# Batch 0 of an attention-plus-MLP kernel: v's cast and q's first normalisation on GpSimd, q and x by head pairs, q's late rows in three pieces

## The chip, the cores and the metric

One core of one Trainium2 chip runs the whole program. The time is the device time of one execution in microseconds (us); before the change its median is 297.52 us. The engines are named as in the profile: PE is TensorE's matmul side and PEld its weight loads, DVE is VectorE, ACT is ScalarE, POOL is GpSimd, and SP is SyncE, which in this kernel only issues DMAs. Each engine takes its instructions in the order of the program.

## The reference

For 8 batches, 8 heads, 576 rows and 64 features, two softmaxes and two small products make x, and a two-layer network with a leaky ReLU follows. Here it is, cut to what is computed:

```python
q_s = exp(q - max(q, axis=-1));  q_s = q_s / (sum(q_s, axis=-1) + 1e-09)   # over the 64 features
k_s = exp(k - max(k, axis=2));   k_s = k_s / (sum(k_s, axis=2) + 1e-09)    # over the 576 rows
kv  = einsum('bhsd,bhse->bhde', k_s, v)
x   = einsum('bhsd,bhde->bhse', q_s, kv).transpose(0, 2, 1, 3).reshape(4608, 512)
h   = x @ w_in                     # 512 x 2048
out = maximum(0.01 * h, h) @ w_out # 2048 x 512
```

## The kernel before, in words

**Layout.** A head's 576 rows are taken as 64 places (`L`) of 9 rows each (`R`). Two heads fill the 128 partitions, and four such `HL` slots hold the batch, so a batch of q, k or v is a tile of 128 x 4 x 9 x 64 in float32. The tokens of a batch are kept in the order r, l, so the first 256 of batch 0's 576 tokens are the rows r = 0 to 3 (`RA`), and the next 256 the rows 4 to 7. x is kept transposed, as `xT`: four blocks of 128 features (a block is a pair of slots `gg` of one partition half `hh`; its number is 2·hh + gg), each with all 4608 tokens.

**The main part.** The tokens go through the network in 9 tiles of 512. For a tile, layer 1 (`layer1`, L452) makes 16 blocks `ph` of 128 hidden features, each from four matmuls over the four blocks of `xT`. ACT applies the leaky ReLU from PSUM to `g` (`leaky`, L461), and layer 2 (`layer2`, L473) makes four outputs `pout` of 128 tokens from 16 matmuls each. In tile 0 a `ph` holds two hidden blocks of 256 tokens, so its layer 1 has 128 matmuls of 256 columns.

**The attention of a batch.** DVE takes maxima (k by a tree, L162, and across partitions; q along the features, L226), DVE or POOL subtracts them (L195, L256), ACT takes the exponential (L203, L264), DVE sums and normalises q (L273, L280), v is cast to bf16 into `vb` (L215), PE makes the key-value products (`kv`, L295), DVE scales them into `kd`, q is transposed (on PE with `q_transpose`, L389, in batches 0 and 1, by DMA later), and `attend` (L412) makes the blocks of x with a copy into `xT`. The work of batches 1 to 7 is hung as hooks (`at(t, u, ...)`) on the matmul groups of an earlier tile, so each engine's order is written out by hand.

**Batch 0** comes ahead of everything, in this order: the loads, q's rows `RA` with a maximum and 16 small exponentials that also give the sums (`q_first`, L239), k's maxima by way of PE, two casts of v on ACT (L213), key-value products, q's transposes, and the first two blocks of x for 256 tokens. `wake(n)` puts n matmuls on zeros (L324) into PE's stream. Then DVE takes the maxima of q's late rows (`R1` is rows 4 and 5, `R2` is rows 6 to 8), and POOL subtracts them (L256).

**Queues.** SP loads q, k and v in the order of use. POOL issues the loads of the weights, which are cast to bf16 on the way: `load_w_in(0)` and `load_w_in(1)` are four pieces each (L133), `load_w_out` five pieces (L140). They are put off by small copies into `gate` that read a tile which must have landed: `w_in` first waits for k's second half (L509), then for its subtraction (L534), and `w_out` waits for the first half of batch 1's k (L564). SP in turn is held by `hold_sync` (L504), a tiny DMA that reads a piece of a weight: batch 1's loads wait for the fifth piece of `w_in`.

**PSUM.** Nearly every PSUM tile comes from one pool of six banks (`psB_pool`), so a new `ph` needs an earlier tile's reader, often a `leaky` on ACT, to be through.

**Tile 0 before.** Four `ph` tiles are begun on `xT`'s blocks 0 and 2, `attend` makes blocks 1 and 3, and then the groups are finished one by one:

```python
attend(0, [1, 3], 0, 256, nc.scalar)
for half in range(2):
    for j in range(0, NF, 2):
        ...
            layer1(j + i, ph[:, i], 256 * half, 256, part, i == 0, i == 1)
            if i == 1:
                leaky(g_sb[j // 2][:, :, 256 * half : 256 * half + 256], ph)
            run(0, 16 * half + j + i)
```

The late rows' exponentials hang on the groups j = 3 and j = 5, so in ACT's stream two `leaky` stand ahead of the first.

Of the kernel before, what the change touches and what calls it, by code (L numbers as in the profile page):

```python
# [25 lines left out]
def kernel(  # L26
# [201 lines left out]
    def q_first(b, rs):  # L228

        n = rs.stop - rs.start  # L230
        nmax = small_pool.tile([P, HL, n], FP32, name="nmax")
        qsum = small_pool.tile([P, n, HL], FP32, name="qsum")
        for hs in (slice(0, 2), slice(2, 4)):
# [3 lines left out]
            for h in range(hs.start, hs.stop):  # L237
                for r in range(n):
                    nc.scalar.activation(  # L239
                        out=st[b]["qe"][:, rs.start + r, h],  # L240
                        in_=st[b]["q"][:, h, rs.start + r],
                        func=AF.Exp,
                        bias=nmax[:, h, r : r + 1],
                        accum_out=qsum[:, r, h : h + 1],
                    )
        st[b]["qsum"] = qsum

    def q_first_rec(b, rs):
        n = rs.stop - rs.start
        st[b]["qrec", rs.start] = qrec = small_pool.tile([P, n, HL], FP32, name="qrec")  # L250
        nc.vector.reciprocal(out=qrec, in_=st[b]["qsum"])

    def q_sub(eng, b, rs):
        n = rs.stop - rs.start
# [67 lines left out]
    def wake(n):  # L322
        for i in range(n):
            nc.tensor.matmul(  # L324
                wake_ps, lhsT=zero[:, 0:P], rhs=zero, start=(i == 0), stop=(i == n - 1)
            )

    def k_max_pe(b, i):
        ps = psB_pool.tile([P, 2, L], FP32, name="kT", tag=BANK_TAG)
        nc.tensor.matmul(  # L330
            ps.rearrange("c h l -> c (h l)"),
            lhsT=st[b]["kmax"][:, 2 * i : 2 * i + 2].rearrange("p h d -> p (h d)"),
            rhs=identf,
            is_transpose=True,
        )
        st[b]["kT", i] = ps
# [154 lines left out]
            fn()  # L491

    H0, H1 = slice(0, 2), slice(2, 4)

    def load_all(b):
        whole = [(ALLH, ALLR)]
# [34 lines left out]
    v_cast(nc.scalar, 0, 0)  # L531
    v_cast(nc.scalar, 0, 1)
    k_sub_ps(0, 1)
    nc.gpsimd.tensor_copy(out=gate[:, 0:1], in_=st[0]["k"][:, HL - 1, R - 1, D - 1 : D])  # L534
    load_w_in(1)
    k_exp(0, H1)
    q_first_rec(0, RA)
    q_norm(0, RA)
    kv_pair(0, 0)
    wake(4)  # L540
    q_transpose(0, 0, 4)
    kv_pair(0, 1)
    for hh in range(2):
        kd_rec(0, 0, hh)
        kd_one(nc.vector, 0, 0, hh)
    q_keep(nc.scalar, 0, 0, 4, slice(0, 4, 2))
    q_keep(nc.vector, 0, 0, 4, slice(1, 4, 2))
    attend(0, [0, 2], 0, 256, nc.scalar)
    wake(3)
    kd_rec(0, 1, 0)  # L550
    kd_rec(0, 1, 1)
    kd_one(nc.vector, 0, 1, 0)
    kd_one(nc.vector, 0, 1, 1)
# [19 lines left out]
    at(0, 11, lambda: q_transpose(0, 4, 2), lambda: q_keep(nc.vector, 0, 4, 2))  # L573
    at(0, 13, lambda: q_transpose(0, 6, 3), lambda: q_keep(nc.vector, 0, 6, 3))
    at(0, 15, lambda: attend(0, [0, 2], 256, 256, nc.scalar))
    at(0, 15, lambda: attend(0, [1, 3], 256, 256, nc.vector))
    at(0, 17, lambda: attend(0, [0, 1, 2, 3], 512, 64, nc.scalar))
    at(0, 15, lambda: k_begin(1), lambda: q_begin(1), lambda: k_tree(1, H0), lambda: k_tree(1, H1))
    at(0, 15, lambda: k_allmax(1), lambda: k_sub(nc.gpsimd, 1, H0), lambda: k_sub(nc.vector, 1, H1))
    at(0, 15, lambda: q_max(1, RA), lambda: q_sub(nc.gpsimd, 1, RA))  # L580
    at(0, 15, lambda: q_max(1, RB), lambda: q_sub(nc.gpsimd, 1, RB))
    at(0, 29, lambda: k_exp(1, H1))
    at(0, 31, lambda: k_exp(1, H0), lambda: v_cast(nc.scalar, 1, 0))
    at(0, 33, lambda: q_exp(1, RA), lambda: q_sum(1, RA), lambda: q_norm(1, RA))
    at(0, 33, lambda: v_cast(nc.scalar, 1, 1), lambda: q_exp(1, RB))
    at(0, 38, lambda: kv(1), lambda: kd_make(1), lambda: q_sum(1, RB), lambda: q_norm(1, RB))
    at(0, 41, lambda: q_transpose(1, 0, 2), lambda: q_keep(nc.scalar, 1, 0, 2))
    at(0, 42, lambda: q_transpose(1, 2, 2), lambda: q_keep(nc.scalar, 1, 2, 2))
    at(0, 45, lambda: q_transpose(1, 4, 3), lambda: q_keep(nc.scalar, 1, 4, 3))
    at(0, 46, lambda: q_transpose(1, 7, 2), lambda: q_keep(nc.scalar, 1, 7, 2))  # L590
# [8 lines left out]
    def plan(b, o):  # L599
        t = b - 2  # L600
        at(t, o, lambda: k_begin(b), lambda: q_begin(b), lambda: k_tree(b, ALLH))
        at(t, o + 3, lambda: k_allmax(b), lambda: k_sub(nc.gpsimd, b, ALLH))
        at(t, o + 7, lambda: q_max(b, ALLR), lambda: q_sub(nc.gpsimd, b, ALLR))
        at(t, o + 11, lambda: k_exp(b, ALLH))
        at(t, o + 12, lambda: v_cast(nc.gpsimd, b, 0), lambda: v_cast(nc.gpsimd, b, 1))
        at(t, o + 16, lambda: q_exp(b, ALLR))
        at(t, o + 18, lambda: q_sum(b, ALLR))
        at(t, o + 21, lambda: q_norm(b, ALLR))
        kvu, pu = o + 25, o + (33 if b == 3 else 34)
        at(t, kvu, lambda: kv(b))  # L610
        at(t, kvu + 1, lambda: kd_make(b))
        at(t, o + 22, lambda: q_turn(b))
        for i in range(8):
            at(t, pu + i // 2, lambda i=i: attend_x(b, i // 2, XR[i % 2], nc.scalar))


    def plan2():
        b = 2
        at(1, 0, lambda: k_begin(b), lambda: q_begin(b), lambda: k_tree(b, ALLH))
        at(1, 3, lambda: k_allmax(b))  # L620
        at(1, 6, lambda: k_sub(nc.vector, b, H0), lambda: k_sub(nc.vector, b, H1))
# [7 lines left out]
        at(1, 21, lambda: kv(b))  # L629
        at(1, 22, lambda: kd_make(b))  # L630
        for i in range(8):
            at(1, 28 + i // 2, lambda i=i: attend_x(b, i % 4, XR[i // 4], nc.scalar))

    plan2()
    for b in range(3, B):
# [4 lines left out]
        return [g_pool.tile([P, 2, TT], BF16, name="gj") for _ in range(NF // 2)]  # L640

    g_sb = g_tiles()
    begun = []
    for j in range(0, 8, 2):
        ph = psB_pool.tile([P, 2, 256], FP32, name="ph", tag=BANK_TAG)
        for i in range(2):
            layer1(j + i, ph[:, i], 0, 256, slice(0, 2), i == 0)
        begun.append(ph)
    attend(0, [1, 3], 0, 256, nc.scalar)
    for half in range(2):  # L650
        for j in range(0, NF, 2):
            part = slice(2, 4) if begun else slice(0, 4)
            ph = begun.pop(0) if begun else psB_pool.tile([P, 2, 256], FP32, name="ph", tag=BANK_TAG)
            for i in range(2):
                layer1(j + i, ph[:, i], 256 * half, 256, part, i == 0, i == 1)
                if i == 1:
                    leaky(g_sb[j // 2][:, :, 256 * half : 256 * half + 256], ph)
                run(0, 16 * half + j + i)
# [66 lines left out]
```

## Time and profile before

| | us |
|---|---|
| median of the runs | 297.52 |
| lowest run | 296.36 |
| span of the profiled execution | 293.0 |
| PE busy in it | 278.8 |
| PE busy on zeros (L324, 26 matmuls) | 8.9 |
| ACT busy, DVE busy, POOL busy | 150.8, 144.9, 85.6 |
| tile 0: layer 1 begins, layer 2 begins | 17.05, 36.14 |
| tile 1: layer 1 begins | 54.28 |

The span runs from the first to the last instruction of one execution, whose own time is not listed apart from it. The median is 4.5 us above the span. A row of the timeline gives the start, the duration, the engine, the line, what is written from what, and in brackets the idle time before it with what ended that. A row that ends in x16 merges 16 instructions. A row of the waits view gives who waited for whom, the total, how often, and the longest.

### The profile page before, as it was taken

The numbers are of one execution on the slowest core, as the hardware profiler recorded it, in microseconds if no ns is written. First come the engines' busy times: TensorE is split into PE (matmuls) and PEld (weight loads), VectorE is DVE, ScalarE is ACT, GpSimd is POOL, SyncE is SP. The second block draws the span as 40 slices with busy tenths as digits, with TensorE's granted clock in tenths as the row PEclk, the third lists the DMA queues.
The fourth block names the chain that finished last, engine by engine and source line by source line (L and its number), as shares of the span: only waits on it lengthen the run. The fifth ranks groups of instructions, "written<-read, shape, count | busy, mean of one in ns | idle before, by whom it ended". The sixth has DMA issues, their size and how long they took to land.

```text
span 293.0 us, 4255 instructions
## 1 busy us (share of the span) xinstructions
PE 278.8 (95%) x1634; PEld 139.1 (47%) x1661; DVE 144.9 (49%) x240; ACT 150.8 (51%) x272; POOL 85.6 (29%) x61
## 2 busy tenths in 40 slices
PE   6596999999999999999999999999999999999995
PEld 2265845444544455454445544544455444444443
DVE  3947957885491597189367455735440200110011
ACT  4956682777058605951695338532854066007500
POOL 4645280025029307802920292029300000000000
PEclk9999999999999999999999999999999999999999
DMA  7999999694729553874399138923141310131032
GB/s 258 307 211 387 247 191 400 160 345 152 135 55 326 196 116 91 273 266 88 70 326 276 36 72 289 294 55 72 38 81 38 72 36 1 38 72 36 0 72 73
DMA packets 36580, 45.76 MB, mean 156 GB/s; under 512 B 15952, under 2 KB 19280, under 8 KB 36560
## 3 DMA queue, kind: packets, MB, share of 16 engines
q1 hardware_dynamic: 33120, 41.16, 47.4%
q0 software_dynamic: 3280, 4.20, 8.2%
q8 instruction: 13, 0.21, 0.3%
q10 hardware_dynamic: 160, 0.13, 0.1%
q14 instruction: 7, 0.06, 0.1%
HBM read 36.70 MB, written 9.44 MB: 157 GB/s over the span
## 4 chain that ended last, share of the span: by engine, by line
PE 84%; DMA 3%; DVE 3%; ACT 2%; POOL 2%; issue 1%; POOLq 0%; ACTq 0%
PE pout L473 40%; PE ph L452 39%; DMA w_in_sb<-in_moe_w_in_dram 3%; PE pkv L295 3%; PE po L440 2%; POOL k_raw L195 1%; DVE t L162 1%; ACT vb L213 1%; DVE k_raw L356 1%; ACT xT L422 1%; PE psum_qt L389 1%; POOL w_in_sb L133 0%; ACT qe L264 0%; DVE xT L424 0%; DVE m L179 0%
## 5 line engine op out<-in xcount | busy, mean ns | idle before, releaser
L452 PE MATMUL ph<-xT,w_in_sb 128*128 128x512 bf16 (+1 forms) x626 | 127.1, 357 | 4.3 <-DMA w_in_sb<-in_moe_w_in_dram 1.9
L473 PE MATMUL pout<-w_out_sb,gj 128*128 128x512 bf16 (+2 forms) x580 | 129.1, 373 | 0.9 <-issue 0.5
L461 ACT ACTIVATE gj<-ph 128x512 bf16<-128x512 f32 x144 | 82.5, 604 | 58.5 <-PE ph L452 57.9
L452 PEld LDWEIGHTS <-w_in_sb 128*128 128x128 bf16 x640 | 62.0, 98 | 66.1 <-issue 5.5
L473 PEld LDWEIGHTS <-gj 128*128 128x128 bf16 x592 | 56.9, 98 | 61.6
L467 DVE COPY out_sb<-pout 128x512 f32<-128x512 f32 (+1 forms) x34 | 22.7, 675 | 90.7 <-PE pout L473 82.1
L195 POOL TENSOR_TENSOR k_raw<-k_raw,kall 128x2304 f32<-128x2304 f32 (+1 forms) x6 | 29.1, 4844 | 86.2 <-DVE kall L187 55.8
L273 DVE TENSOR_REDUCE qsum<-qe 128x36 f32<-128x2304 bf16 (+4 forms) x11 | 19.8, 1800 | 39.5 <-ACT qe L264 39.5
L256 POOL TENSOR_TENSOR q_raw<-q_raw,qmax 128x2304 f32<-128x2304 f32 (+4 forms) x11 | 31.1, 2839 | 23.5 <-DVE qmax L226 23.5
L446 ACT CAST xT<-po 128x320 bf16<-128x320 f32 (+1 forms) x48 | 16.8, 402 | 40.0 <-PE po L440 40.0
L203 ACT ACTIVATE ke<-k_raw 128x2304 bf16<-128x2304 f32 (+2 forms) x11 | 17.5, 1595 | 9.7 <-POOL k_raw L195 9.4
L280 DVE TENSOR_TENSOR qe<-qe,qrec 128x2304 bf16<-128x2304 bf16 (+4 forms) x12 | 21.1, 1758 | 0.4
L226 DVE TENSOR_REDUCE qmax<-q_raw 128x36 f32<-128x2304 f32 (+4 forms) x11 | 19.4, 1788 | 0.0
L264 ACT ACTIVATE qe<-q_raw 128x2304 bf16<-128x2304 f32 (+4 forms) x11 | 16.9, 1535 | 0.0
L215 POOL CAST vb<-v_raw 128x1152 bf16<-128x1152 f32 x12 | 13.4, 1151 | 0.0
L467 ACT COPY out_sb<-pout 128x512 f32<-128x512 f32 (+1 forms) x3 | 1.6, 549 | 17.5 <-PE pout L473 17.5
L162 DVE TENSOR_TENSOR t<-k_raw 128x1024 f32<-128x1024 f32 (+1 forms) x10 | 10.1, 1010 | 0.4 <-DMA k_raw<-in_k_dram 0.2
L324 PE MATMUL pout<-zero 128*128 128x512 bf16 x26 | 8.9, 469 | 1.4 <-POOL zero L101 1.3
L162 DVE TENSOR_TENSOR t<-t 128x256 f32<-128x256 f32 (+2 forms) x20 | 9.6, 478 | 0.7
L440 PE MATMUL po<-qX,kd 128*128 128x320 bf16 (+1 forms) x48 | 9.8, 286 | 0.1
L295 PEld LDWEIGHTS <-ke 64*128 64x128 bf16 x252 | 7.2, 93 | 3.2 <-ACT gj L461 1.7
L295 PE MATMUL pkv<-vb,ke 64*128 64x129 bf16 x252 | 8.5, 216 | 0.1
(55 smaller groups left out, 103.5 us busy)
## 6 DMA issues: line engine op xcount, KB each, us to landing
out_dram<-out_sb SPq DMA_DIRECT2D x70, 128.0 KB, 2.4
q_raw<-in_q_dram SPq DMA_DIRECT2D x7, 1152.0 KB, 8.2
v_raw<-in_v_dram SPq DMA_DIRECT2D x7, 1152.0 KB, 11.0
k_raw<-in_k_dram SPq DMA_DIRECT2D x6, 1152.0 KB, 5.8
k_raw<-in_k_dram SPq DMA_DIRECT2D x4, 576.0 KB, 5.6
w_in_sb<-in_moe_w_in_dram POOLq DMA_DIRECT2D x8, 256.0 KB, 7.4
w_out_sb<-in_moe_w_out_dram POOLq DMA_DIRECT2D x3, 512.0 KB, 12.2
v_raw<-in_v_dram SPq DMA_DIRECT2D x2, 576.0 KB, 7.4
```

What stands on the lines that cost most here:

```text
L162: nc.vector.tensor_tensor(out=o, in0=i0, in1=i1, op=ALU.max)
L195: eng.tensor_tensor(out=ks, in0=ks, in1=st[b]["kall"][:, hs].unsqueeze(2).to_broadcast([P, n, R, D]), op=ALU.subtract,)
L203: nc.scalar.activation(out=st[b]["ke"][:, :, hs].rearrange("p r h d -> p h r d"), in_=st[b]["k"][:, hs], func=AF.Exp,)
L226: nc.vector.tensor_reduce(out=m, in_=st[b]["q"][:, :, rs], axis=AX.X, op=ALU.max)
L256: eng.tensor_tensor(out=qs, in0=qs, in1=st[b]["qmax", rs.start].unsqueeze(3).to_broadcast([P, HL, n, D]), op=ALU.subtract,)
L273: nc.vector.reduce_sum(out=qsum, in_=st[b]["qe"][:, rs], axis=AX.X)
L280: nc.vector.tensor_tensor(out=qes, in0=qes, in1=st[b]["qrec", rs.start].unsqueeze(3).to_broadcast([P, n, HL, D]), op=ALU.mult,)
L295: nc.tensor.matmul(pkv[hh][:, gg, 0:129], lhsT=st[b]["ke"][rows, r, 2 * gg : 2 * gg + 2].rearrange("p h d -> p (h d)"), rhs=vb2[b % 2][row ...
L452: nc.tensor.matmul(ph, lhsT=w_in_sb[:, cb, j * P : (j + 1) * P], rhs=xT[:, cb, c0 : c0 + n], start=(i == 0 and first), stop=(i == NB - 1 a ...
L461: nc.scalar.activation(out=o, in_=ph, func=AF.Prelu, alpha=LEAKY_SLOPE)
L467: copy(out=out_sb, in_=pout)
L473: nc.tensor.matmul(pout, lhsT=g_sb[j // 2][:, j % 2, tsub * P : (tsub + 1) * P], rhs=w_out_sb[:, j, os], start=(j == 0), stop=(j == NF - 1),)
```

## The change

The change concerns batches 0 to 3; the other hooks stay.

- v's two casts of batch 0 go from ACT to POOL, behind a `gate` copy that waits for k's last maximum.
- q's rows `RA` are normalised by head pairs: one reciprocal each on DVE, one multiplication each on POOL, where one reciprocal and one multiplication on DVE stood. They are also transposed, kept and attended by pairs.
- The first `w_in` gate waits for k's first half instead of its second. `load_w_in(1)` stands behind the casts and multiplications on POOL.
- `hold_sync` reads a piece of block 1 instead of block 0, so SP waits for the seventh `w_in` piece.
- Tile 0's first half is begun in two groups of four `ph`, part by part. Between parts stand the attends of blocks 1 and 3, the late rows' maxima and subtractions (`x1`), and two transposes.
- The late rows are cut in three (4 and 5, 6 and 7, 8). Their exponentials hang on j = 0, 3 and 13.
- Of batches 1 to 3, casts, exponentials, key-value products and attends move by some hooks. Zero matmuls go from 27 to 23.

The diff, cut to its core:

```diff
-    R1, R2 = slice(4, 6), slice(6, R)
+    R1, R2, R3 = slice(4, 6), slice(6, 8), slice(8, R)
...
+    def q_first_rec(b, gg):
+        st[b]["qrec2", gg] = qrec = small_pool.tile([P, RA.stop, 2], FP32, name="qrec2")
+        nc.vector.reciprocal(out=qrec, in_=st[b]["qsum", gg])
+
+    def q_first_norm(eng, b, gg):
+        qes = st[b]["qe"][:, RA, 2 * gg : 2 * gg + 2]
+        eng.tensor_tensor(
+            out=qes,
+            in0=qes,
+            in1=st[b]["qrec2", gg].unsqueeze(3).to_broadcast([P, RA.stop, 2, D]),
+            op=ALU.mult,
+        )
...
-    nc.gpsimd.tensor_copy(out=gate[:, 0:1], in_=st[0]["k"][:, HL - 1, R - 1, D - 1 : D])
+    nc.gpsimd.tensor_copy(out=gate[:, 0:1], in_=st[0]["k"][:, 1, R - 1, D - 1 : D])
     load_w_in(0)
...
+    nc.gpsimd.tensor_copy(out=gate[:, 0:1], in_=st[0]["kmax"][:, HL - 1, D - 1 : D])
+    v_cast(nc.gpsimd, 0, 0)
+    v_cast(nc.gpsimd, 0, 1)
...
-    wake(2)
+    wake(3)
+    q_first_rec(0, 0)
+    q_first_norm(nc.gpsimd, 0, 0)
     k_sub_ps(0, 0, HB)
     k_exp(0, slice(1, 2))
-    v_cast(nc.scalar, 0, 0)
-    v_cast(nc.scalar, 0, 1)
+    q_first_rec(0, 1)
+    q_first_norm(nc.gpsimd, 0, 1)
+    load_w_in(1)
     k_sub_ps(0, 1)
...
+    q_turn_first(0, 0)
+    q_keep_first(nc.vector, 0, 0)
...
+    attend(0, [0], 0, 256, nc.scalar)
     kv_pair(0, 1)
+    attend(0, [2], 0, 256, nc.scalar)
+    q_turn_first(0, 1)
+    q_keep_first(nc.scalar, 0, 1)
...
-    q_max(0, R1)
-    q_sub(nc.gpsimd, 0, R1)
-    q_max(0, R2)
-    q_sub(nc.gpsimd, 0, R2)
...
-    hold_sync(0, w_in_sb[0:1, 0, F - 128 : F])
+    hold_sync(0, w_in_sb[0:1, 1, F - 128 : F])
     st[1]["k"] = load(k, 1, "k_raw", [(H0, ALLR), (H1, ALLR)])
...
     nc.gpsimd.tensor_copy(out=gate[:, 0:1], in_=st[1]["k"][:, 0, 0, 0:1])
     for j0, j1 in ((0, 2), (2, 4), (4, 8), (8, 12), (12, 16)):
         load_w_out(slice(j0, j1))
...
-    at(0, 3, lambda: q_exp(0, R1), lambda: q_sum(0, R1), lambda: q_norm(0, R1))
-    at(0, 5, lambda: q_exp(0, R2), lambda: q_sum(0, R2), lambda: q_norm(0, R2))
...
+    def q_rest(rs):
+        q_exp(0, rs)
+        q_sum(0, rs)
+        q_norm(0, rs)
+
+    at(0, 0, lambda: q_rest(R1))
+    at(0, 3, lambda: q_rest(R2))
+    at(0, 13, lambda: attend(0, [0, 2], 256, 256, nc.scalar))
+    at(0, 13, lambda: attend(0, [1, 3], 256, 256, nc.vector))
+    at(0, 13, lambda: q_rest(R3))
+    at(0, 17, lambda: q_transpose(0, 8, 1), lambda: q_keep(nc.scalar, 0, 8, 1))
...
-        at(0, 47, lambda i=i: attend(1, [i // 2], 288 * (i % 2), 288, nc.scalar))
+        at(0, (45, 45, 46, 46, 46, 47, 47, 47)[i], lambda i=i: attend(1, [GS[i // 2]], 288 * (i % 2), 288, nc.scalar))
...
+    def begin(js, parts):
+        phs = [psB_pool.tile([P, 2, 256], FP32, name="ph", tag=BANK_TAG) for _ in js]
+        for i, between in parts:
+            for j, ph in zip(js, phs):
+                for h in range(2):
+                    layer1(j + h, ph[:, h], 0, 256, slice(i, i + 1), h == 0, False)
+            for fn in between:
+                fn()
+        return phs
+
+    def end(j, ph, half, part, first):
+        for h in range(2):
+            layer1(j + h, ph[:, h], 256 * half, 256, part, first and h == 0, h == 1)
+            if h == 1:
+                leaky(g_sb[j // 2][:, :, 256 * half : 256 * half + 256], ph)
+            run(0, 16 * half + j + h)
+
+    def x1():
+        attend(0, [1], 0, 256, nc.scalar)
+        attend(0, [3], 0, 256, nc.vector)
+        for rs in (R1, R2, R3):
+            q_max(0, rs)
+            q_sub(nc.gpsimd, 0, rs)
+
+    t1 = (lambda: q_transpose(0, 4, 2), lambda: q_keep(nc.scalar, 0, 4, 2))
+    t2 = (lambda: q_transpose(0, 6, 2), lambda: q_keep(nc.vector, 0, 6, 2))
+    for j0, parts in ((0, ((0, (x1,)), (1, ()))), (8, ((0, t1), (1, t2)))):
+        js = range(j0, j0 + 8, 2)
+        for j, ph in zip(js, begin(js, parts)):
+            end(j, ph, 0, slice(2, 4), False)
+    for j in range(0, NF, 2):
+        end(j, psB_pool.tile([P, 2, 256], FP32, name="ph", tag=BANK_TAG), 1, slice(0, 4), True)
```

More of the change, by code (lines that the diff above doesn't have):

```diff
@@ L231, in q_first @@
         nmax = small_pool.tile([P, HL, n], FP32, name="nmax")
-        qsum = small_pool.tile([P, n, HL], FP32, name="qsum")
-        for hs in (slice(0, 2), slice(2, 4)):
+        for gg in range(2):
+            hs = slice(2 * gg, 2 * gg + 2)
+            st[b]["qsum", gg] = qsum = small_pool.tile([P, n, 2], FP32, name="qsum2")
             nc.vector.tensor_reduce(
@@ L236, in q_first, with q_turn_first, q_keep_first @@
             )
-            for h in range(hs.start, hs.stop):
+            for h in range(2):
                 for r in range(n):
                     nc.scalar.activation(
-                        out=st[b]["qe"][:, rs.start + r, h],
-                        in_=st[b]["q"][:, h, rs.start + r],
+                        out=st[b]["qe"][:, rs.start + r, 2 * gg + h],
+                        in_=st[b]["q"][:, 2 * gg + h, rs.start + r],
                         func=AF.Exp,
-                        bias=nmax[:, h, r : r + 1],
+                        bias=nmax[:, 2 * gg + h, r : r + 1],
                         accum_out=qsum[:, r, h : h + 1],
                     )
[L246 to L251, printed above, removed]
+    def q_first_rec(b, gg):
[9 more added lines that the diff above has]
+        )
+    def q_turn_first(b, gg):
+        n = RA.stop
+        ps = psB_pool.tile([P, 2, n, L], BF16, name="psum_q2", tag=BANK_TAG)
+        for r in range(n):
+            nc.tensor.matmul(
+                ps[:, :, r],
+                lhsT=st[b]["qe"][:, r, 2 * gg : 2 * gg + 2].rearrange("p h d -> p (h d)"),
+                rhs=ident,
+                is_transpose=True,
+                start=(r == 0),
+                stop=(r == n - 1),
+            )
+        st[b]["ps2", gg] = ps
+    def q_keep_first(eng, b, gg):
+        o, i = st[b]["qT"][:, gg::2, RA], st[b]["ps2", gg]
+        if eng is nc.scalar:
+            eng.copy(out=o, in_=i)
+        else:
+            eng.tensor_copy(out=o, in_=i)
     def q_sub(eng, b, rs):
@@ L493 @@
     H0, H1 = slice(0, 2), slice(2, 4)
+    GS = (0, 2, 1, 3)
     def load_all(b):
@@ L527 @@
     k_all_pe(0, 1)
[L528 removed]
+    wake(3)
+    q_first_rec(0, 0)
+    q_first_norm(nc.gpsimd, 0, 0)
     k_sub_ps(0, 0, HB)
     k_exp(0, slice(1, 2))
[L531 to L532 removed]
+    q_first_rec(0, 1)
+    q_first_norm(nc.gpsimd, 0, 1)
+    load_w_in(1)
     k_sub_ps(0, 1)
[L534 to L535 removed]
     k_exp(0, H1)
[L537 to L538 removed]
     kv_pair(0, 0)
[L540 to L541 removed]
+    wake(2)
+    kd_rec(0, 0, 0)
+    kd_one(nc.vector, 0, 0, 0)
+    q_turn_first(0, 0)
+    q_keep_first(nc.vector, 0, 0)
+    kd_rec(0, 0, 1)
+    kd_one(nc.vector, 0, 0, 1)
+    attend(0, [0], 0, 256, nc.scalar)
     kv_pair(0, 1)
+    attend(0, [2], 0, 256, nc.scalar)
+    q_turn_first(0, 1)
+    q_keep_first(nc.scalar, 0, 1)
     for hh in range(2):
[L544 to L553, printed above, removed]
[L554 to L560 removed]
+        kd_rec(0, 1, hh)
+        kd_one(nc.vector, 0, 1, hh)
+    hold_sync(0, w_in_sb[0:1, 1, F - 128 : F])
     st[1]["k"] = load(k, 1, "k_raw", [(H0, ALLR), (H1, ALLR)])
@@ L591 @@
+    at(0, 33, lambda: q_sum(1, RB))
+    at(0, 41, lambda: kv(1))
+    at(0, 41, lambda: q_norm(1, RB), lambda: kd_make(1))
+    for r0 in (0, 2):
+        at(0, 41, lambda r0=r0: q_transpose(1, r0, 2), lambda r0=r0: q_keep(nc.scalar, 1, r0, 2))
+    for r0, n in ((4, 3), (7, 2)):
+        at(0, 43, lambda r0=r0, n=n: q_transpose(1, r0, n), lambda r0=r0, n=n: q_keep(nc.scalar, 1, r0, n))
     for i in range(8):
-        at(0, 47, lambda i=i: attend(1, [i // 2], 288 * (i % 2), 288, nc.scalar))
+        at(0, (45, 45, 46, 46, 46, 47, 47, 47)[i], lambda i=i: attend(1, [GS[i // 2]], 288 * (i % 2), 288, nc.scalar))
@@ L642 @@
     g_sb = g_tiles()
[L643 to L658, printed above, removed]
+    def begin(js, parts):
[8 more added lines that the diff above has]
+    def end(j, ph, half, part, first):
+        for h in range(2):
+            layer1(j + h, ph[:, h], 256 * half, 256, part, first and h == 0, h == 1)
[16 more added lines that the diff above has]
+        end(j, psB_pool.tile([P, 2, 256], FP32, name="ph", tag=BANK_TAG), 1, slice(0, 4), True)
     pout = [psO_pool.tile([P, O], FP32, name="pout") for _ in range(2)]
```

26 lines of the change are left out of this document (8 added, 18 removed).

## The prediction

> **What bounds the kernel now.** I read the page first, then the chain by line, then PE's waits and the timeline of the first 55 us.
>
> ```profile
> span 293.0 us, 4255 instructions
> PE 278.8 (95%) x1634; PEld 139.1 (47%) x1661; DVE 144.9 (49%) x240; ACT 150.8 (51%) x272; POOL 85.6 (29%) x61
> PE 84%; DMA 3%; DVE 3%; ACT 2%; POOL 2%; issue 1%; POOLq 0%; ACTq 0%
> ```
>
> PE carries the end: 278.8 of 293.0 us busy, and 84% of the chain. Whatever delays PE after layer 1 has begun (17.05) is added to the end one for one, unless a later wait of PE absorbs it. PE's waits from 16 to 45 us are few:
>
> ```profile
> PE ph L452 <- DMA w_in_sb<-in_moe_w_in_dram: 1.9, 1, 1.9
> PE ph L452 <- ACT xT L422: 1.4, 2, 0.7
> PE pout L473 <- issue: 0.2, 1, 0.2
> ```
>
> So 3.5 us is all that a better order could win there. The timeline shows in which order POOL and ACT serve this stretch:
>
> ```profile
> 16.41 0.58 ACT L422 CAST xT<-po 128x512 bf16<-128x512 f32 x1 [0.47 <-PE po L412]
> ...
> 17.80 2.47 POOL L256 TENSOR_TENSOR q_raw<-q_raw,qmax 128x512 f32<-128x512 f32 x2 [2.54 <-DVE qmax L226]
> ...
> 19.37 0.62 SPq L504 DMA_DIRECT2D held<-w_in_sb  x1
> ...
> 20.03 1.08 SPq L79 DMA_DIRECT2D k_raw<-in_k_dram  x2
> 20.48 1.08 ACT L461 ACTIVATE gj<-ph 128x512 bf16<-128x512 f32 x2 [0.69 <-PE ph L452]
> ...
> 21.45 0.63 ACT L264 ACTIVATE qe<-q_raw 128x512 bf16<-128x512 f32 x1
> ...
> 23.89 1.69 PE L452 MATMUL ph<-xT,w_in_sb 128*128 128x256 bf16 x14 [1.92 <-DMA w_in_sb<-in_moe_w_in_dram]
> ...
> 25.51 0.41 POOL L564 COPY gate<-k_raw 128x1 f32<-128x1 f32 x1 [5.24 <-DMA k_raw<-in_k_dram]
> ...
> 25.97 3.71 POOL L140 DMA_DIRECT2D w_out_sb<-in_moe_w_out_dram  x5
> ```
>
> The reader is to see POOL's order: the late rows' subtractions at 17.80, then 5.24 us of waiting for batch 1's k, then the w_out loads until 29.68. ACT takes two leaky ahead of the first late exponential (21.45).
>
> **The change part by part.** Times are on the clock of this one execution; its span is 293.0, the median 297.52, so I carry 4.5 us over.
>
> *Up to layer 1.* ACT loses two casts (2 x 1.14), DVE a multiplication of 1.22 us; POOL gets two casts (1.15 each, the L215 row), two multiplications, and a second gate copy (0.19 to 0.41). k's last maximum ends at 9.88, so the casts end near 12.5. Before, the first key-value product waited 1.44 us for v, until 13.22; now it starts at about 12.6. A multiplication of 512 elements per partition in bf16 on POOL is not in the trace: DVE's takes 0.69, POOL's subtraction of 128x512 in float32 1.04; and POOL's k subtraction of 1152 took 3.73 beside a DVE subtraction, against 5.07 for 2304, so 1.47 times longer, which gives 1.53. I take 1.04, the same engine and size; the ends are 0.69 and 1.53. The second multiplication ends at 14.6 (13.9 to 15.6). The two transposes, copies (0.42, 0.58) and attends by pairs then let layer 1 begin near 16.1 instead of 17.05. The GPSIMD Engine Reference (Trainium skill, 8. Key points) says GpSimd contends with VectorE instructions that have two SBUF inputs; by it the end at 1.53 would hold, and the 3.73 us row agrees. These 0.9 us are worth nothing to the end, since PE next waits for weights or for ACT. In the same way DVE's second reciprocal (0.16 to 0.25) and the extra PSUM tiles cost nothing: that wait covers them, and without it they would take at most 0.5 us off the 0.9.
>
> *w_in.* The second four loads are issued from 14.6 instead of 12.88, behind the casts and multiplications. Before, SP's hold went out at 19.37, when the fifth piece landed; the seventh, issued at 14.04, landed 7.9 us later, at 21.9. The shortest landing of a load of this size is 3.9 us (q's first), so a fifth piece issued at 14.6 to 15.6 can land at 18.5 to 19.5: the stream stays full and the seventh still lands near 22.0 (up to 23.0). The new hold waits for it; its row and the next put k's load 0.66 later, at 22.7. The k load took 5.4 behind w_in and q's first load 3.9; I take 4.2, as one w_in piece is still ahead. Batch 1's k lands at 26.9 (25.9 to 28.5) instead of 25.4. On SP's queue batch 1's q and v stand behind it and move by the same 1.5 to 2.6 us, as do w_out's landings, which share the DMA engines, and behind them batch 2's loads, held by a w_out piece. Layer 2 comes later by more than that (below) and batch 2 is first touched in tile 1, so this costs nothing; if layer 2 were not late, w_out's first pieces would be the next thing PE waits for.
>
> *POOL's queue.* This part decides. The late rows' subtractions used to stand ahead of the gate copy. `x1` is called from tile 0's loop, so they now stand behind the gate and the five w_out loads. From the gate to the end of the loads took 4.17 us (25.51 to 29.68), so R1's subtraction starts at 26.9 + 4.2 = 31.1, ends at 32.1, and ACT's exponential (0.63) ends at 32.8.
>
> *ACT's queue.* R1's exponential now hangs on j = 0 and stands ahead of the first leaky. ACT is idle from about 17.7 on, and all leaky wait behind it; the first ends at 33.4 (0.60). DVE waits as well, with its sum of R1; nothing behind it is due yet.
>
> *PE.* It goes on without ACT as long as PSUM has banks: 32 matmuls of the first group, and after w_in's sixth piece (20.6) four more of the second. The third `ph` of that group needs the bank that the first leaky frees. PE stands from about 21.2 to 33.45, 12.2 us, where before it stood 1.92.
>
> *From there to layer 2.* Of 128 matmuls 92 are left: 0.109 each (56 in 6.28 less the last one's tail) is 10.0. Ten transposes at 0.06 and the late attends (4 x 0.11, 4 x 0.03) are 1.2. Short waits: R1's normalisation (0.69 + 0.20 + 0.69 after 32.8) holds its transposes by 0.5; xT after the attends costs 0.7 as at 29.04; R3's short chain 0.7. Together 1.9. Zero in, this gives 46.5.
>
> *Clock.* Here the trace shows only two cases: after the 1.92 us gap 14 matmuls took 1.69, so nothing was lost; and at the start PE ran at half its rate for 3.8 us:
>
> ```profile
> 4.70 0.15 PEld L324 LDWEIGHTS <-zero 128*128 128x128 bf16 x1 [0.28 <-issue]
> 5.13 0.80 PEld L324 LDWEIGHTS <-zero 128*128 128x128 bf16 x4 [0.28 <-issue]
> ```
>
> Weight loads 0.43 apart, then 0.20. A 12 us pause is nearer to the start than to 1.92: 3.8 us less some 0.8 us of waits in it, at half rate, costs 1.5 (0 to 1.9). The granted clock reads 1.00 at the start too, so it will not show it. TensorE: Matmul & The Clock Gate (Trainium skill, Part 1) states that an idle window of about 3.4 us halves the clock until 3.4 us of work have passed; by it the cost would be about 1.7. Layer 2 begins at 48.0 instead of 36.14: +11.9.
>
> *Given back.* Layer 2 of tile 0 took 18.14 (36.14 to 54.28). Its PE work is 64 x 0.216 + 1.13 for the key-value products + 18 x 0.06 + 8 x 0.12 = 17.0; with attends now spread over three groups its waits mostly go: 17.2, so -0.9. Batch 1 keeps up: DVE's tree starts near 41.5 and took 14.1 us to the products (28.96 to 43.07), so 55.6, and the new hook (group 41) comes at 48.0 + 9 x 0.86 = 55.8. The moves in batches 2 and 3 touch waits of 0.11 to 0.16 each: -0.4 in all (-0.6 to +0.5). Fewer zero matmuls free PE while it waits: 0.
>
> Sum: +11.9 - 0.9 - 0.4 = +10.6, a span of 303.6 and a time of 308.1.
>
> **Rivals.**
>
> 1. *Longer:* the gate opens late (28.5) and batch 1's chain, with 0.2 us of slack, is late too, by up to 2 us. +1.6 alone gives 309.7, with the 2 us 311.7. For it: that slack. Against it: the stages after it have layer 2 work to fill.
> 2. *GpSimd only delays w_in:* ACT is not held, and the eighth piece lands 1.5 us late, at 25.3. PE then has 80 matmuls left (8.7) + 1.2 + 1.4 of waits: layer 2 at 36.6, +0.5, less 1.3 given back: 296.7, or 298 if nothing is given back. For it: the loads do move behind 4.4 us of POOL work. Against it: the stream was full from 12 to 22 us, and the order above.
> 3. *Not slower:* POOL reaches R1's subtraction before about 19, because the copy that waits for batch 1's k does not hold what follows it. Then PE fills the w_in wait with 14 matmuls and two transposes more, and after the eighth piece at 23.5 come 80 matmuls (8.7), 1.2 and 1.9: layer 2 at 35.3, -0.8 - 1.3: 295.4, or 296.7 if nothing is given back. It decides at this point: the subtraction must end by 20.0, or ACT's first leaky comes after PE has run out of banks at 21.2. Against it: that copy held POOL for 5.24 us in the trace, and the subtractions come after it in program order.
>
> **How the numbers follow.** The forecast has 0.80, with 304.5 to 310 as its own range: low end k at 25.9 (-1.0), no clock cost (-1.5) and the w_out loads beside less traffic (-1); high end the bounds of the multiplications and k (+1.6). Rival 1 has 0.11, rival 2 0.05, rival 3 0.04. The range 304.5 to 311.5 leaves out rivals 2 and 3 and the edges. About 2% (6 us, so 303.5) is what a measurement of this kernel can tell from no change: slower 0.91, within 2% 0.08, faster by 2% 0.01, since PE's waits that could go do not amount to 6 us.
>
> **What would show it.** Right: a PE wait of 11 to 13 us at L481 (layer 1's new line) ending near 33 on ACT's leaky; ACT idle from about 17.7 until 32 on POOL's subtraction; POOL's w_out loads ahead of the subtractions; the hold near 22.0. Half rate after the pause shows as 256-column matmuls 0.21 apart. Wrong: ACT's first leaky before 22, or layer 2 of tile 0 beginning before 44.

## The result, and the profile after

The change makes the kernel slower: the median of its four runs is 306.53 us (305.96 to 307.46), and the ratio to the kernel before is 1.0362, with a 95% interval of 1.0329 to 1.0396. Of the kernel before there are four runs beside them (297.52, 1044.59, 296.36, 295.96); the one of 1044.59 is a slow run, which the ratio leaves out, and the median of the other three is 296.36. The profiled execution took 305.96 us, of which its span is 304.2. From the page of the kernel after, the span, the busy times, the slices of PE and of its clock, and the chain by engine:

```profile
span 304.2 us, 4282 instructions
PE 280.4 (92%) x1657; PEld 139.1 (46%) x1657; DVE 146.0 (48%) x244; ACT 149.3 (49%) x274; POOL 90.2 (30%) x66
PE   5760589999999999999999999999999999999995
PEclk9996599999999999999999999999999999999999
PE 86%; DMA 5%; POOL 3%; ACT 2%; DVE 2%; issue 1%; SPq 0%; POOLq 0%
```

PE is busy only 1.6 us longer than before; the other 9.6 us of the span's 11.2 are time in which it stands. They lie in one place: the fourth slice (22.8 to 30.4 us) has a 0 for PE, and the granted clock reads 6 and 5 tenths in it and the next. From the seventh slice on PE is at 9 again. Layer 2 of tile 0 begins 12.45 us later (48.59 against 36.14), layer 1 of tile 1 11.43 later (65.71 against 54.28), and the last layer 2 11.2 later: all is lost before 48.6, and 1.2 given back behind it. PE's waits from 12 to 70 us, after (who waits for whom, total, times, longest):

```profile
PE ph L481 <- ACT gj L490: 11.8, 1, 11.8
PE ph L481 <- DMA w_in_sb<-in_moe_w_in_dram: 1.9, 1, 1.9
PE ph L481 <- ACT xT L451: 0.6, 2, 0.4
```

The wait for weights is as long as before. The new one is 11.8 us on a leaky of ACT. The timeline of after shows the chain that ends in it:

```profile
21.39 0.60 PE L481 MATMUL ph<-xT,w_in_sb 128*128 128x256 bf16 x4 [1.87 <-DMA w_in_sb<-in_moe_w_in_dram]
22.67 0.63 SPq L534 DMA_DIRECT2D held<-w_in_sb  x1
23.34 1.08 SPq L79 DMA_DIRECT2D k_raw<-in_k_dram  x2
...
27.37 0.19 POOL L593 COPY gate<-k_raw 128x1 f32<-128x1 f32 x1 [10.49 <-DMA k_raw<-in_k_dram]
27.82 3.70 POOL L140 DMA_DIRECT2D w_out_sb<-in_moe_w_out_dram  x5 [0.27 <-issue]
31.50 2.65 POOL L285 TENSOR_TENSOR q_raw<-q_raw,qmax 128x512 f32<-128x512 f32 x3
32.62 0.63 ACT L293 ACTIVATE qe<-q_raw 128x512 bf16<-128x512 f32 x1 [15.43 <-POOL q_raw L285]
33.16 1.07 ACT L490 ACTIVATE gj<-ph 128x512 bf16<-128x512 f32 x2
...
33.79 1.07 PE L481 MATMUL ph<-xT,w_in_sb 128*128 128x256 bf16 x4 [11.80 <-ACT gj L490]
```

Read it from the end. PE waits for a leaky, which stood on ACT behind the late rows' exponential; that waited 15.43 us for POOL's subtraction; POOL was issuing the five `w_out` loads, and before them it stood 10.49 us at the gate copy for batch 1's k, whose load SP sent when the seventh `w_in` piece had landed. DVE had the maxima of the first late rows ready soon after 17.27, so the subtraction was delayed by nothing but its place in POOL's queue.

### The profile page after: what moved, and what is told of

The parts are those of the page before. It is cut to its first block, busy times and chain, and to the rows that moved or that the text cites. A ratio compares the mean times of both kernels' runs of the same rounds, so it can differ in the third digit from the quotient of the medians.

```text
span 304.2 us, 4282 instructions
## 1 busy us (share of the span) xinstructions
PE 280.4 (92%) x1657; PEld 139.1 (46%) x1657; DVE 146.0 (48%) x244; ACT 149.3 (49%) x274; POOL 90.2 (30%) x66
## 4 chain that ended last, share of the span: by engine, by line
PE 86%; DMA 5%; POOL 3%; ACT 2%; DVE 2%; issue 1%; SPq 0%; POOLq 0%
PE pout L502 41%; PE ph L481 39%; DMA k_raw<-in_k_dram 3%; PE pkv L324 3%; DMA w_in_sb<-in_moe_w_in_dram 2%; PE po L469 2%; POOL w_out_sb L140 1%; ACT gj L490 1%; DVE t L162 1%; PE psum_qt L418 1%; POOL vb L215 1%; POOL qe L254 1%; ACT xT L451 0%; ACT qe L293 0%; POOL w_in_sb L133 0%
## 5 line engine op out<-in xcount | busy, mean ns | idle before, releaser
L481 PE MATMUL ph<-xT,w_in_sb 128*128 128x512 bf16 (+1 forms) x640 | 129.7, 361 | 14.3 <-ACT gj L490 11.8
L293 ACT ACTIVATE qe<-q_raw 128x2304 bf16<-128x2304 f32 (+4 forms) x12 | 17.1, 1426 | 16.1 <-POOL q_raw L285 16.1
L203 ACT ACTIVATE ke<-k_raw 128x2304 bf16<-128x2304 f32 (+2 forms) x11 | 17.4, 1594 | 9.3 <-POOL k_raw L195 8.5
L215 POOL CAST vb<-v_raw 128x1152 bf16<-128x1152 f32 x14 | 15.7, 1150 | 0.0
L353 PE MATMUL pout<-zero 128*128 128x512 bf16 x23 | 7.3, 450 | 1.3 <-POOL zero L101 1.3
L342 DVE TENSOR_TENSOR kd<-pkv,krec 64x128 bf16<-64x128 f32 x28 | 8.1, 289 | 0.7
```

Source lines behind the costliest of these rows:

```text
L203: nc.scalar.activation(out=st[b]["ke"][:, :, hs].rearrange("p r h d -> p h r d"), in_=st[b]["k"][:, hs], func=AF.Exp,)
L215: eng.tensor_copy(out=o, in_=i)
L481: nc.tensor.matmul(ph, lhsT=w_in_sb[:, cb, j * P : (j + 1) * P], rhs=xT[:, cb, c0 : c0 + n], start=(i == 0 and first), stop=(i == NB - 1 a ...
```

## The experiments

The first theory: the late rows' subtractions stand behind a gate copy that waits for a transfer, and this order on GpSimd is the whole loss. Rivals: that the exponential now stands ahead of the first leaky on ACT is enough by itself (e7); that the later hold is the cause (e3); that GpSimd's added work, by way of `w_in`, is (e1, which keeps all of it). All but e2 start from the kernel after, and where two times or a ratio stand, the second is the kernel before beside them on the same chip; the chips differ from group to group, so times of different groups are compared by their ratios. The maxima stay where they are unless said.

**e1_order: the gate copy, the `w_out` loads, the next hold and batch 2's loads behind the subtractions.**

```diff
-    nc.gpsimd.tensor_copy(out=gate[:, 0:1], in_=st[1]["k"][:, 0, 0, 0:1])
-    for j0, j1 in ((0, 2), (2, 4), (4, 8), (8, 12), (12, 16)):
-        load_w_out(slice(j0, j1))
-    hold_sync(1, w_out_sb[0:1, 11, 0:128])
-    load_all(2)
+    def w_out_later():          # the same five lines
...
             q_sub(nc.gpsimd, 0, rs)
+        w_out_later()           # at the end of x1
```

> The changed kernel, except that the gate copy that waits for batch 1's k, the five w_out loads and what SP issues behind them are called at the end of x1, so on GpSimd the late rows' subtractions stand ahead of the gate again. Theory (GpSimd's queue order makes the stall): the 11.8 us PE wait on ACT's first leaky goes, layer 2 of tile 0 begins near 35.5 to 36.5, and the time is 294.5 to 296 us, at or a little under the kernel before. Rival 1 (GpSimd's casts and multiplications, which put w_in's second half behind them, are the cost): these are unchanged, so the time stays at 304 to 307. Rival 2 (the later hold of batch 1's loads is the cost): also unchanged, 304 to 307.

Measured: 296.55 against 296.03, ratio 1.0006 [0.998, 1.0033]; span 293.6. From its timeline:

```profile
18.44 2.61 POOL L285 TENSOR_TENSOR q_raw<-q_raw,qmax 128x512 f32<-128x512 f32 x3 [1.50 <-DVE qmax L226]
19.51 0.63 ACT L293 ACTIVATE qe<-q_raw 128x512 bf16<-128x512 f32 x1 [1.91 <-POOL q_raw L285]
...
27.79 0.19 POOL L594 COPY gate<-k_raw 128x1 f32<-128x1 f32 x1 [6.74 <-DMA k_raw<-in_k_dram]
...
37.52 3.61 PE L502 MATMUL pout<-w_out_sb,gj 128*128 128x512 bf16 x16 [2.30 <-DMA w_out_sb<-in_moe_w_out_dram]
```

The subtraction is through 12 us sooner and the 11.8 us wait is gone, with every other part of the change still in. The order alone makes the loss. But the time is above the forecast of 294.5 to 296, and layer 2 begins at 37.52, not at 35.5 to 36.5. The last row shows what stands behind that: PE waits 2.30 us for `w_out`'s first piece, since the gate opened only at 27.79.

**e2_before_behind: the same fault alone, put into the kernel before.** Its maxima and subtractions of the late rows are written behind the gate and the loads.

```diff
-    q_max(0, R1)
-    q_sub(nc.gpsimd, 0, R1)
-    q_max(0, R2)
-    q_sub(nc.gpsimd, 0, R2)
...
     load_all(2)
+    q_max(0, R1)
+    q_sub(nc.gpsimd, 0, R1)
+    q_max(0, R2)
+    q_sub(nc.gpsimd, 0, R2)
```

> The kernel before, with one edit: the late rows' maxima and subtractions are written after the gate copy and the w_out loads instead of ahead of the hold. Theory (queue order): the subtraction begins near 29.7 instead of 17.8, PE waits 6 to 8 us for the late rows' transposes or for a bank, its clock then restarts at half rate, and the time is 303 to 305.5. Rival 1 (GpSimd's new work) and rival 2 (the later hold): neither is in this kernel, so the time stays at 296.5 to 298.

Measured: 304.96, ratio 1.0306 [1.0273, 1.0339]. From its timeline and PE's waits:

```profile
25.14 0.18 POOL L560 COPY gate<-k_raw 128x1 f32<-128x1 f32 x1 [9.60 <-DMA k_raw<-in_k_dram]
25.60 3.69 POOL L140 DMA_DIRECT2D w_out_sb<-in_moe_w_out_dram  x5 [0.28 <-issue]
29.27 2.52 POOL L256 TENSOR_TENSOR q_raw<-q_raw,qmax 128x512 f32<-128x512 f32 x2
```

```profile
PE psum_qt L389 <- DVE qe L280: 7.5, 1, 7.5
```

The move alone costs 3%, as forecast. The wait is shorter, 7.5 us, and has another name: the exponentials still stand behind two leaky there, so ACT frees banks and PE gets as far as the late rows' transposes.

**e3_hold5 and e5_between: the parts of the stall.** One puts the hold back on the fifth piece; the other puts the subtractions between the gate copy and the `w_out` loads.

```diff
# e3_hold5
-    hold_sync(0, w_in_sb[0:1, 1, F - 128 : F])
+    hold_sync(0, w_in_sb[0:1, 0, F - 128 : F])
# e5_between: the gate copy stays, the loads move behind the subtractions
-    for j0, j1 in ((0, 2), (2, 4), (4, 8), (8, 12), (12, 16)):
-        load_w_out(slice(j0, j1))
-    hold_sync(1, w_out_sb[0:1, 11, 0:128])
-    load_all(2)
...
             q_sub(nc.gpsimd, 0, rs)
+        w_out_later()
```

> The changed kernel, with the hold of batch 1's loads back on w_in's fifth piece. Theory (queue order; the stall ends when batch 1's k lands plus 4.2 us of gate and loads plus 2.3): the hold goes out near 19 instead of 22.7, the k lands at 25.4 to 25.8 instead of 27.3, and the time falls by 1.5 to 2.0, to 304.5 to 305. Rival 2 (the later hold is the main cost): 297 to 299. Rival 1: 306.5, unchanged.

> The changed kernel, with the late rows' subtractions between the gate copy and the five w_out loads: still behind the wait for batch 1's k, but no longer behind the 3.7 us of issuing the loads. Theory (the stall is the sum of both): the first leaky comes 3.7 to 4.1 us earlier, PE's long wait falls from 11.8 to about 7.9, and the time falls to 302.3 to 303.0. If issuing the loads does not hold what follows on GpSimd, the time stays at 306.5; if the wait for k is harmless, it falls to 296.

Measured: e3 305.39, ratio 1.0332 [1.0292, 1.0371]; e5 302.40, ratio 1.0236 [1.0201, 1.0271]. In e3 the hold goes out 3.6 us sooner (19.05), but k lands only 1.1 sooner (26.16): issued while `w_in`'s last pieces are under way, it takes 6.44 us instead of 3.90, and `w_in`'s seventh piece lands at 23.36 instead of 22.65. PE's wait is 11.15, and PE restarts at 32.70 instead of 33.79. So the hold gives 1.1 us, less than was expected of it. In e5 the time is as forecast, and the wait is 8.04:

```profile
27.91 0.19 POOL L593 COPY gate<-k_raw 128x1 f32<-128x1 f32 x1 [11.19 <-DMA k_raw<-in_k_dram]
28.06 2.61 POOL L285 TENSOR_TENSOR q_raw<-q_raw,qmax 128x512 f32<-128x512 f32 x3
29.13 0.63 ACT L293 ACTIVATE qe<-q_raw 128x512 bf16<-128x512 f32 x1 [12.08 <-POOL q_raw L285]
```

So some 3.8 of the 11.8 us are the issue of the five loads (3.70 in after, with 0.27 ahead of it). The rest is the wait for k, which landed 0.54 later in e5 than in after, and the short chain behind it.

**e4_warm: matmuls on zeros inside the stall.** 52 matmuls on zeros are put ahead of the third `ph` of the second group, so PE is busy where it stood.

```diff
             for j, ph in zip(js, phs):
+                if (i, j) == (0, 12):
+                    wake(52)
```

> The changed kernel with 52 matmuls on zeros put into PE's stream where it runs out of PSUM banks, so that PE works through 11.2 us of the pause instead of standing; the output is the same. If the pause costs clock as well (PE at half rate for 4.4 us after it), the granted clock stays at 1.00, 256-column matmuls stand 0.11 apart after the pause, and the time falls by 1.2 to 2.0, to 304.5 to 305.3. If the half rate costs nothing because the work there waits for ACT and VectorE anyway, the time stays within 0.4 of 306.5.

Measured: 305.78, ratio 1.0339 [1.031, 1.0367]. The granted clock stays at 1.00. From PE's restart to layer 2 it takes 13.61 us (34.24 to 47.85) instead of 14.80 (33.79 to 48.59; 14.85 in e3 and 14.80 in e5, which also restart at half rate). The stretch view gives us, PE, PEld, DVE, ACT and POOL busy, the granted clock, the DMA share and GB/s; first of after, split where its clock comes back, then of e4:

```profile
33.70:38.19 4.49, 3.99 (x22) 2.74 (x22) 2.81 (x7) 2.60 (x6) 0.45 (x1) 0.50 1.18 248
38.19:48.58 10.39, 9.50 (x90) 8.16 (x88) 7.98 (x21) 7.66 (x15) 1.64 (x1) 1.00 1.06 228
```

```profile
34.20:47.85 13.65, 11.97 (x111) 9.90 (x111) 10.75 (x28) 10.21 (x20) 2.06 (x2) 1.00 1.14 226
```

PE needs 13.49 us of work in after and 11.97 in e4 for the same stretch, so half rate cost 1.5 us of PE time; 0.3 of it came back as shorter waits, and 1.2 was left. The profiled execution gains only 0.73 (305.23 against 305.96), because in it k landed later, the gate copy came at 27.82 instead of 27.37, and the restart 0.45 later. The medians are 0.75 apart, between the two forecasts, and their ratios' intervals overlap; so the cost of the half rate rests on the stretches of the traces, not on the medians.

**e7_dve: the subtractions on VectorE**, with the exponentials' places on ACT and the gate's on POOL as in the change.

```diff
             q_max(0, rs)
-            q_sub(nc.gpsimd, 0, rs)
+            q_sub(nc.vector, 0, rs)
```

> The changed kernel, with the late rows' subtractions on VectorE instead of GpSimd; GpSimd's order is left as the change has it. Theory (the stall comes from standing behind the gate on GpSimd, not from the exponential's place in ACT's stream): the 11.8 us wait goes, a wait for w_out of about 2 us comes, and the time is 296 to 297.5. If the place of the exponential ahead of ACT's first leaky is the cause by itself, PE still waits over 5 us and the time stays over 301.

Measured: 295.56 against 294.97, ratio 0.9998 [0.9975, 1.002], a little under the forecast of 296 to 297.5. From its timeline:

```profile
18.24 0.69 DVE L285 TENSOR_TENSOR q_raw<-q_raw,qmax 128x512 f32<-128x512 f32 x1
18.97 0.63 ACT L293 ACTIVATE qe<-q_raw 128x512 bf16<-128x512 f32 x1 [1.52 <-DVE q_raw L285]
...
27.16 0.19 POOL L593 COPY gate<-k_raw 128x1 f32<-128x1 f32 x1 [10.43 <-DMA k_raw<-in_k_dram]
```

POOL stands at the gate as long as in the change, and the 11.8 us wait is gone. An exponential ahead of the first leaky does no harm once its input comes in time, so that rival falls. PE waits 1.6 us for `w_out` in three pieces and layer 2 begins at 35.96.

**e6_order_hold5 and e8_wout_first: what holds e1.** e6 is e1 with the hold on the fifth piece. e8 is e1 with the first two `w_out` loads issued right behind `load_w_in(1)`, ahead of any gate.

```diff
# e6_order_hold5, against e1
-    hold_sync(0, w_in_sb[0:1, 1, F - 128 : F])
+    hold_sync(0, w_in_sb[0:1, 0, F - 128 : F])
# e8_wout_first, against e1
     load_w_in(1)
+    load_w_out(slice(0, 2))
+    load_w_out(slice(2, 4))
```

> The first experiment (subtractions ahead of the gate) with the hold of batch 1's loads back on w_in's fifth piece. In the first experiment PE then waited 2.3 us for w_out's first piece at the start of layer 2. If that is because all loads of batch 1 stand ahead of w_out and start 3.7 us later than before the change, that wait falls by 1.0 to 1.3 and the time to 295.0 to 295.6. If w_out's landing depends on its own issue alone, it stays at 296.5.

> The first experiment with w_out's first two pieces issued right behind w_in's second half, ahead of batch 1's loads; the other three stay behind the gate. If the 2.3 us wait at the start of layer 2 is what took the gain of the change back, it goes, batch 1's k lands 1 to 2.5 us later, and the time falls by 1.0 to 2.3, to 294.3 to 295.5. If the later k then makes batch 1's key-value products late, the time stays at 296 to 297.

Measured: e6 293.27 against 294.97, ratio 0.9942 [0.9921, 0.9963]; e8 294.82, ratio 0.9979 [0.9956, 1.0003]. In e6 the gate opens at 26.39, layer 2 begins at 35.75 without a wait, which is more than was forecast, and PE's waits for `w_in` grow from 1.15 and 0.62 to 1.38 and 1.77 us. In e8 layer 2 begins at 34.25, the earliest of all, but the loads put ahead of batch 1's k push that to 28.47, and PE waits later, 0.64 us for `w_out` at 38.50 and 1.01 us at 48.26 for batch 1's chain:

```profile
PE psum_qt L418 <- DVE kd L342: 1.0, 1, 1.0
```

**e9_wake18 and e10_cast_act: two parts of the change, from e6.** e9 adds four zero matmuls at the start; e10 gives v's casts back to ACT.

```diff
# e9_wake18
-    wake(14)
+    wake(18)
# e10_cast_act
-    v_cast(nc.gpsimd, 0, 0)
-    v_cast(nc.gpsimd, 0, 1)
...
     k_exp(0, slice(1, 2))
+    v_cast(nc.scalar, 0, 0)
+    v_cast(nc.scalar, 0, 1)
```

> The sixth experiment (subtractions ahead of the gate, hold on the fifth piece; 293.3 us) with 18 instead of 14 matmuls on zeros at the start, so that PE stands for less time before k's first transpose. In some runs the granted clock fell to half for 3.4 us from about 9 on, after a stand of some 2.4 us. If that is what spreads the runs by 1 to 2 us, the clock stays at 1.00 from about 6 on, and the median falls by 0.3 to 1.0, to 292.3 to 293.0. If the head's clock costs nothing because PE waits there anyway, it stays at 293.0 to 293.6.

> The sixth experiment with v's two casts back on ACT, in their place before the change; the multiplications stay on GpSimd. Layer 1 begins 0.5 to 1.5 us later, near 16.5. By the prediction's step that the earlier begin is worth nothing, since PE next waits for w_in, the time stays at 293.0 to 293.8. If the casts on GpSimd are what makes the sixth experiment faster than the kernel before, it rises to 294.3 to 295.5. If w_in's second half, now issued 2.3 us sooner, lands sooner, it falls to 292.0 to 292.8.

Measured, on one chip: e9 293.85, ratio 0.9945 [0.9925, 0.9965]; e10 292.43 against 295.14, ratio 0.9905 [0.9884, 0.9926]. The zeros bring nothing; in e9's trace the clock falls not near 9 us but at 22.26, behind a wait of 2.98 us for `w_in`. In e10 layer 1 begins 0.8 us later than in e6 (16.38), yet PE does not wait for `w_in` at all, since its second half is issued at 12.90 instead of 14.39 and lands from 18.71 to 23.58 instead of 19.18 to 25.02, as the third theory had it. The stretch from 16 to 22 us, in e6 and in e10:

```profile
16.00:22.00 6.00, 4.62 (x45) 3.83 (x44) 4.46 (x9) 3.73 (x8) 3.44 (x5) 1.00 1.07 177
```

```profile
16.00:22.00 6.00, 5.46 (x51) 4.26 (x47) 4.29 (x11) 3.38 (x8) 2.61 (x3) 1.00 1.12 213
```

The last number is GB/s: 177 with the casts on POOL (185 in after), 213 without (211 in the kernel before). With the late issue the transfers did not stay full.

**e11_win_first and e12_e6_again, on one chip.** e11 is e10 with `load_w_in(1)` ahead of POOL's two multiplications; e12 is e6 unchanged.

```diff
# e11_win_first, against e10
+    load_w_in(1)
...
     q_first_norm(nc.gpsimd, 0, 1)
-    load_w_in(1)
```

> This is e10 (subtractions ahead of the gate, hold on the fifth piece, v's casts on ScalarE) with the four loads of w_in's second half issued on GpSimd ahead of its two q multiplications. First theory: with the casts gone the stream of w_in is already full in e10 (its fifth to eighth pieces land 18.71 to 23.58), so loads issued 2.2 us sooner land no sooner, layer 2 begins at 34.4 to 34.8 as in e10, and the time is 292.0 to 292.8. Rival: the multiplications, then ending at 15 to 15.4, put layer 1's begin later by 0.5 to 1 (16.9 to 17.4 against 16.38), and 292.7 to 293.5 results.

> The kernel of e6 once more, unchanged (v's casts on GpSimd), on the same chip as e11, to compare the places of the casts on one chip. If moving the casts to ScalarE gains what e6 and e10 showed on two chips, this run is 0.6 to 1.1 us above e11, at 293.0 to 293.6; if that was the chips' difference, the two lie within 0.3.

Measured: e11 293.06 against 295.89, ratio 0.9914 [0.9881, 0.9947]; e12 293.32, ratio 0.9924 [0.9893, 0.9955]. In e11 the loads are issued at 10.51 and the fifth piece lands at 18.61, 0.1 us sooner than in e10, and layer 2 begins at 34.69: the stream was full already, as the first theory had it. The median of e11 lies in the rival's range all the same, but not by the rival's step: layer 1 begins at 16.44, not at 16.9 to 17.4. Against e12 the gain is 0.26, which by the expectation speaks for a difference between the chips, and the intervals overlap. So the medians do not settle whether the casts' place is worth anything. The traces differ (in e12 PE waits 3.2 us for `w_in`, in e11 not at all), and so do the runs with a mean granted clock of 0.998 and above: a median of 292.08 for e11 (4 runs) and of 292.65 for e12 (5 runs); but that was not what the runs were made for.

The best by its median is e10, the change with the gate and the `w_out` loads behind the subtractions, the hold on the fifth piece and v's casts on ScalarE: 0.95% faster than the kernel before beside it, a gain of 2.7 us where the change as made loses 10.2. e11, with a like time on another chip, is not told apart from it.

## Why the prediction was right, point by point

The mechanism was as forecast, and the two rivals without a held ACT fell: after shows ACT held for 15.43 us, and e1 has the added POOL work and no loss. The terms, and where they were off:

- *Up to layer 1* (forecast 16.1): 15.63. The multiplications took 1.05 and 1.04, the middle value. DVE subtracted k beside the first of them, so the end of 1.53 did not come. The GPSIMD Engine Reference (Trainium skill, 8. Key points) limits its contention to DVE instructions with two SBUF inputs or in a 2-port mode; that DVE subtraction reads one input from PSUM, so these multiplications do not test the rule. The row of 3.73 us from which 1.53 came can also be read as a sum instead of a factor: half of 5.07 is 2.54, and DVE's subtraction ran 1.24 us more beside it (34.93 to 36.29, from POOL's start at 35.05). As said, the gain was worth nothing: PE stood 1.87 us for `w_in` instead.
- *`w_in`* ("the stream stays full and the seventh still lands near 22.0"): this step failed by 0.65. The fifth piece landed at 18.98 and the sixth at 21.25, 2.27 us apart where the others come 1.07 to 1.57 apart and before all but the last came 1.2 to 1.3 apart; the seventh came at 22.65. A landing time of a single load (3.9 us) said when the fifth could be there, not that the sixth would follow at once. It does not: in the ten traces with the late issue (casts on POOL, fifth piece issued at 14.27 to 14.79) the sixth lands 1.29 to 3.43 us behind the fifth, and in the four with the earlier one (before, e2, e10, e11; 10.51 to 13.17) 1.25 or 1.26. PE's first wait for `w_in` is longest where that gap is: 3.23 us in e12 and 2.98 in e9, against 1.21 in e8.
- *k's load*: issued at 23.34, 0.64 later than forecast for that reason, landed after 3.9 us instead of 4.2. The gate came at 27.37 (forecast 26.9), inside the bounds; rival 1's 28.5 was not reached.
- *POOL's and ACT's queues*: from the gate to the subtraction 4.13 (4.17), the subtraction 1.09, the exponential 0.63; the first leaky ended near 33.8 (33.4). e5 shows some 3.8 us of issue by itself.
- *The wait*: 11.8 us until 33.79 (12.2 until 33.45).
- *To layer 2*: 14.80 (14.55), from terms that were off in both directions. PE's work at full clock was 12.0 (e4) instead of 11.2: 0.109 each holds in a long run (40 matmuls from 43.48 to 47.85 in e4), but the short runs that end in a wait keep their tail (the first four took 0.87 there, eight after 39.98 took 1.03). The waits were 1.3 (0.42, 0.40, 0.49) instead of 1.9. Half rate cost 1.5 of PE's time, as forecast, though 1.2 net.
- *"The granted clock … will not show it"* was wrong. It reads 0.50 from 24.53 to 38.19, and the page's PEclk row shows it at once. The 1.00 over the slow weight loads at the very start was misread: the trace of before holds no clock record ahead of 5.22, just where the loads come closer, and a stretch without a record reads as 1.00.
- *Given back*: layer 2 of tile 0 took 17.12 (17.2). Batch 1's products came at 57.32 without a wait of PE (forecast: they keep up). Behind tile 1 0.2 instead of 0.4.
- *The sum*: +11.2 of span against +10.6.
- *The 4.5 us carried from span to median* were the largest error. 297.52 is the middle one of 296.36, 297.52 and 1044.59, so a single run far off made the higher of the two others the median. In every execution that has both numbers, the time is 1.72 to 1.87 above the span. The profiled execution of before therefore took about 294.8. On its own time the forecast would have been 303.6 + 1.8 = 305.4 against 305.96; the 308.1 came from carrying a difference between executions as if it belonged to each. The range of 304.5 to 311.5 carries the same error; moved down by 2.7 it would still hold the measured time. The times differ by 10.2 (306.53 less 296.36), the two spans by 11.2.
- *"If layer 2 were not late, w_out's first pieces would be the next thing PE waits for"*: e1 shows it, with 2.30 us, and e7 with 1.6. Rival 3's 35.3 for layer 2 overlooked it: e1 begins layer 2 at 37.52.

What stays open: the worth of the casts' place on one chip, and why, with the late issue, `w_in`'s sixth piece comes so unevenly behind the fifth.

## What to carry to other kernels

Here GpSimd's queue, which issues transfers behind a gate, was blocked for everything written after it (e1, e2, e7). So before moving compute past such a gate, look up how long the gate copy waits (here 5.24 us before the change, 10.49 after) and add the issue of the loads behind it. When a wait is removed, ask for the next one in the same place: after the order was mended, waits for `w_out`, for `w_in` and for batch 1's chain came up in turn, and the best version gained under 3 us. And make the sum against the time of the execution whose rows are used, never against a median of others, least of all one of three runs that holds one far off.

## What the runs showed of the hardware

The granted clock moves in steps of one length. Its half-rate stretches in the profiled executions lasted 13.65 us (after, e3), 10.24 (e2, e5) and 3.41 (e1, e3, e7, e9, e12), which are four, three and one times 3.41; the last few us of an execution are left out here. In after it fell 2.5 us after PE stopped and came back 4.4 us after the restart. TensorE: Matmul & The Clock Gate (Trainium skill, Part 1) states a free-running window of about 3.4 us, and the lengths agree with it. It calls the window that halves the clock idle; here it need not be. In e12 PE stood for 3.2 us, until 22.74. From its stretch view, the window ahead of the fall and the one behind:

```profile
20.55:23.96 3.41, 1.22 (x14) 1.14 (x15) 2.20 (x5) 1.52 (x4) 0.00 (x0) 1.00 1.05 226
23.96:27.37 3.41, 3.41 (x21) 2.52 (x19) 0.42 (x1) 1.02 (x2) 0.19 (x1) 0.50 1.03 358
```

PE worked 1.22 of 3.41 us in that window, and the next ran at half rate. In after, the window with 0.60 was followed by half rate and the one with 1.80 (17.71 to 21.12) was not. All fourteen traces can be cut into such windows, each from its first clock record on. At full rate, windows with 0.15 to 1.33 us of PE work were all followed by half rate, and those with 1.62 or more never. In between it was mixed (1.44 in e2 was not followed by it, 1.57 in e1 and 1.61 in e7 were), so the work in one window does not decide alone there. A window at half rate was the last one if it held 2.99 us of PE work or more, and not if it held 2.62 or less. So it seems to be where a wait of 2 to 3 us falls in the window that decides whether it also costs half rate. This goes with a spread that was not expected: of 29 runs of the kernel before on one chip, 10 with a mean granted clock that leaves no such window in it (0.998 and above) have a median of 294.77, and 17 with about one window (0.992 to 0.994) 295.82. That one window costs this 1.05 us is not shown: six of the 17 lie between 294.64 and 295.15, two runs with about two windows took 295.76 and 295.85, and the one experiment on the zeros at the start (e9) moved nothing.
